# Sparse attention into a gated feed-forward on one core: batch 2's key transposes and value sums moved, two weight loads and two products halved

## The chip, the core and the metric

The kernel runs on one core of a Trainium2 chip. The core has TensorE (PE, with PEld for its weight loads), VectorE (DVE), ScalarE (ACT), GpSimd (POOL), SyncE (SP) and 16 DMA engines that all queues share. The metric is the time of one execution on the device in microseconds (us). A lower time is better.

## What is computed

Four batches, eight heads, 768 positions, head size 64. Each query attends to the positions nearer than 16 and to one summary per block of 32 positions: the key summary is the maximum over the block, the value summary the mean. The heads' outputs are put side by side into rows of 512 and go through a feed-forward with 2048 hidden units.

```python
k_sum = k.reshape(B, H, nb, block, D).max(axis=3)
v_sum = v.reshape(B, H, nb, block, D).mean(axis=3)
scores_l = np.where(np.abs(pos[:, None] - pos[None, :]) < 16, scale * q @ k.T, -1e9)
scores_s = scale * q @ k_sum.T + np.log(32)
a = softmax(concat([scores_l, scores_s]))
x = a @ concat([v, v_sum])
h = x @ w_in
out = (h * sigmoid(1.702 * h)) @ w_out
```

## The kernel before

The kernel is one long program in which each engine keeps the order in which its instructions are written; nothing reorders them. The order is written by hand, as lists of short step names.

**Stages of one batch.** A batch needs its keys, queries and values loaded, keys and queries turned (head size onto the partitions), the block maxima of the keys and the block sums of the values, then scores, exponential, mask, product with the values, normalization and a turn back. Then comes its feed-forward: the *hidden stage* (16 tiles of 128 hidden units, in two halves of 384 positions, each four matmuls and one gelu on ScalarE) and the *output stage* (21 products of 8 matmuls, three 128-row tiles t with seven products each, in the manner of Strassen, so that VectorE first makes sums of the gelu outputs (`gs`) and of the weights (`ws`)). `seq` orders those products; batch 0 has a shorter list `seq0`. The attention of batch b + 1 is laid beside the output stage of batch b: after each product the function `beside(b + 1, slot)` issues the steps that a table has for that slot, `plan1` for batch 1 and `plan` for the others.

**Names of the steps.** In `plan1` and `plan`: `s` scores of a pair of heads for one half, with the exponential; `m` mask; `v` values of two pairs; `x` turn back on TensorE, `d` by DMA; `t` query and `k` key transposes on TensorE; `j` block maxima and copies of keys (`rest_k`); `K`, `Q`, `V` loads of batch 2; `X` key transposes by DMA on SP's queue (`xk`); `R` the value sums (`value_rows`); `e` and `g` fetch ScalarE's table for the exponential or the gelu. In `XR`, the list for batch 0's second half: `m`, `l`, `o`, `r` hidden tiles; `y` the gelu of an `m` tile; `Pti` product i of tile t; `w`, `G`, `h` sums for the output stage.

**Value sums.** `value_rows(s)` issues on SP four copies of neighbouring rows within the value tile `vw[s]` (`vw<-vw`), 48 small matmuls on TensorE (`vsum`, tile ps_vs) that need all twelve value loads of the batch, five operations on VectorE (`block_sums`: vpart, vs), and on SP two copies of the sums into `vw[s]` (`vw<-vs`). The `v` steps read what these copies wrote. In batch 1's hidden stage it is issued for batch 2 at

```python
if n // 2 == (6 if b == 1 else 1):
    value_rows(s)
```

that is, behind 14 of 16 hidden tiles. For batch 3 it stands behind the first four tiles.

**Buffers.** Scores, transposes on TensorE, values and value sums share two PSUM buffers (`psb`); hidden tiles and products share three in batch 0 and four after it (`pmm`). Keys and queries are loaded into two buffers each (`kb`, `qb`).

**Queues.** POOL issues all loads from HBM, in order, and also makes the masks and some key copies. SP issues the stores of the output and all copies and transposes by DMA, in order. Weight loads: `w_in` in five parts, the last of them columns 1536 to 2048, and `w_out` in four quarters.

Of the kernel before, what the change touches and what calls it, by code (L numbers as in the profile page):

```python
# [35 lines left out]
def kernel(  # L36
# [10 lines left out]
    B, H, S, D = q.shape  # L47
# [196 lines left out]
        wi = moe_w_in.rearrange("(ko ki) n -> ki ko n", ki=128)  # L244
        pool.dma_start(out=w_in_sb[:, :, n0:n1], in_=wi[:, :, n0:n1])

    def load_w_out(rows, cols):
        n, m = NT // 2, d_model // 2
        wo = moe_w_out.rearrange("(nt ni) d -> ni nt d", ni=128)
        pool.dma_start(out=w_out_sb[:, rows * n:rows * n + n, cols * m:cols * m + m],  # L250
                       in_=wo[:, rows * n:rows * n + n, cols * m:cols * m + m])

    def copy(eng, out, in_):
        if eng is act:
# [502 lines left out]
        gelu("CBAE".index(bank) % 2, j + (NT // 2 if bank in "AE" else 0), ff_now[j, bank])  # L757


    def product(b, t, what):  # L760
        n = NT // 2
        l = slice(t * 128, t * 128 + 128)
        r = slice(HALF + t * 128, HALF + t * 128 + 128)
        lo, hi = slice(0, N1), slice(N1, d_model)
        raw_l, raw_r = gTb[:, :, l], gTb[:, :, r]
        w1, w2 = w_out_sb[:, 0:n], w_out_sb[:, n:]
        lhs, rhs, bank, opens = {
            1: (raw_l[:, 0:n], w1[:, :, lo], "A", True),
            2: (raw_l[:, n:], w2[:, :, lo], "C", True),
            6: (gs[:, 1, :, l], ws[:, 1], "A", False),  # L770
            5: (gs[:, 0, :, l], ws[:, 0], "B", True),
            7: (raw_r[:, 0:n], ws[:, 2], "A", False),
            3: (gs[:, 2, :, l], w2[:, :, hi], "B", False),
            4: (raw_r[:, n:], ws[:, 3], "A", False)}[what]
        if opens and b == 0 and bank == "A" and t == 0:
            now["left"] = pleft.tile([128, 512], F32, name="poA", tag="left")
        if opens:
            now[t, bank] = (last_bank("B" if bank == "A" and t == 2 else {"A": "A", "B": "E", "C": "C"}[bank],
                                      "po" + bank) if b + 1 == B
                            else now["left"] if b == 0 and bank == "A" and t < 2  # L780
                            else pmm.tile([128, 512], F32, name="po" + bank, tag="mm"))
        o = N1 if b == 0 and bank == "A" and t == 1 else 0
        po = now[t, bank][:, o:o + N1]
        for i in range(n):
            pe.matmul(out=po, lhsT=lhs[:, i], rhs=rhs[:, i], start=(opens and i == 0 and not o),
                      stop=(i == n - 1), skip_group_check=True)

        def keep_it(name):
            if b + 1 == B and name == "s1":
                t_ = now[t, name] = spare[:, 2 * HALF + t * N1:2 * HALF + (t + 1) * N1]  # L790
            else:
                t_ = now[t, name] = snap.tile([128, N1], F32, name=name, tag=name)
            copy(dve if t == 0 and 0 < b < B - 1 else act, t_, po)

        def give(o, cols, name):
            if (t, o) not in now:
                now[t, o] = outp.tile([128, d_model], F32, name="osb", tag="osb")
            if name:
                dve.tensor_tensor(out=now[t, o][:, cols], in0=po, in1=now[t, name], op=ALU.add)
            else:  # L800
                act.activation(out=now[t, o][:, cols], in_=po, func=ACT.Copy)

        def store(o, tok, cols=slice(0, d_model)):
            r0 = b * S + tok
            sp.dma_start(out=out[r0:r0 + 128, cols], in_=now[t, o][:, cols])
            if cols.start == 0:
                now.pop((t, o))

        last = b == B - 1 and t == JH - 1

        if what == 1 and (b or t == 2):
            keep_it("s1")
        elif what == 1:
            pass
        elif what == 2:
            give("o1", lo, "s1")
        elif what == 6:
            keep_it("s2")
        elif what == 5:
            keep_it("s5")  # L820
        elif what == 7:
            give("o2", hi, "s5")
            if last:
                store("o2", HALF + t * 128, hi)
        elif what == 3:
            give("o1", hi, "s2")
            store("o1", t * 128)
        else:
            give("o2", lo, None)
            store("o2", HALF + t * 128, lo if last else slice(0, d_model))  # L830
# [56 lines left out]
    w50 = vw[0].rearrange("p (j e) h c -> p j e h c", e=2)  # L887
    for a in range(NP):
        load_q1(a)
    load_w_in(1536, 2048)  # L890
    load_w_out(0, 0)
    load_w_out(1, 0)
    load_w_out(0, 1)
    finish_masks()
# [100 lines left out]
    for e in range(2):  # L995
# [4 lines left out]
    load_batch(1)  # L1000


    plan1 = {0: ['j0'], 1: ['j1'], 2: ['t1', 'e', 'K0'], 3: ['R', 'j2', 'K1'], 4: ['s00', 'Q0'], 5: ['s01', 's10', 'j3'], 6: ['m00', 'm01'], 7: ['t2', 's11', 'm10'], 8: ['t3', 'm11', 'Q1', 'V'], 9: ['s02', 's03'], 10: ['m02', 'm03'], 11: ['s12', 's13', 'X0'], 12: ['g', 'v00', 'v01'], 15: ['x00', 'm12'], 16: ['x01', 'm13', 'X1']}
    XE = {}

    plan = {-1: ["s00", "s01"], 2: ["m00", "m01"], 3: ["s02", "s03"], 5: ["m02", "m03", "s10", "s11"],
            7: ["m10", "m11", "s12", "s13"], 9: ["m12", "m13"], 10: ["v00", "v01"], 11: ["d00"],
            12: ["d01"], 13: ["v10", "v11"], 14: ["d10"], 15: ["d11"], 18: ["g"]}

    def beside(b, slot):  # L1010
        for what in (plan1 if b == 1 else plan).get(slot, ()):
            half, i = int(what[1:2] or 0), int(what[-1:] if len(what) > 1 else 0)
            if what[0] == "t":
                tq(i, 1, act)
            elif what[0] == "j":
                rest_k(i, 1, dve if i == 3 else pool)
            elif what[0] == "k":
                tk(i, 1, act)
            elif what[0] == "K":
                load_turned(k, 2, kb2, "kb", (i,))  # L1020
            elif what[0] == "Q":
                load_turned(q, 2, qb2, "qb", (i,))
            elif what[0] == "V":
                load_v(2)
            elif what[0] == "X":
                xk(i, 0)
            elif what[0] == "Y":
                xq(i, 0)
            elif what[0] == "m":
                mask(half, i)  # L1030
            elif what[0] == "g":
                gelu_soon()
            elif what[0] == "R":
                value_rows(1)
            elif what[0] == "e":
                exp_soon()
            elif what[0] == "s":
                scores(b, half, i)
            elif what[0] == "v":
                values(b, half, i)  # L1040
            elif what[0] == "d":
                dx(half, i)
            else:
                tx(half, i, XE.get((half, i), act))
# [11 lines left out]
    def run(steps):  # L1056

        for what in steps.split():
# [4 lines left out]
                scores(0, 1, i)  # L1063
                mask(1, i)
            elif what[0] == "P":
                product(0, i, int(what[2]))
            elif what[0] == "v":
                values(0, 1, i)
            elif what[0] == "x":
# [19 lines left out]
            elif what[0] == "N":  # L1089
                held[what[1:]] = pleft.tile([128, 512], F32, name="ph", tag="left")[:, 0:HALF]  # L1090
                ff_step(held[what[1:]], 0, int(what[1:]))
            elif what[0] == "y":
                gelu(0, int(what[1:]), held.pop(what[1:]))
            elif what[0] == "K":
                k_late(i, dve)
                key_halos(i, 0, dve, JH)
                key_rows(i, 0, ks0[:, i, 0:nb], dve, JH)
            elif what[0] == "C":
                dve.memset(vw[1][:, :, :, D:VC], 1.0)
                clear_values(dve, 1)  # L1100
            elif what[0] == "V":
                act.activation(out=gate3[:, 0:1], in_=gate[:, 0:1], func=ACT.Copy)
                vrows0()
            elif what[0] == "w":
                w_sum(i, int(what[2]))
            elif what[0] == "G":
                g_sums(i, dve, (0, 2, 1, 3), int(what[2]))
            elif what[0] == "h":
                g_sums(i, dve, (0, 1))
            elif what[0] == "k":  # L1110
                tk(i, 1, act)
            elif what[0] == "j":
                rest_k(i, 1, pool)
            elif what[0] == "t":
                tq(i, 1, act)
            else:
                value_rows(1)
# [4 lines left out]
    snap = ctx.enter_context(tc.tile_pool(name="snap", bufs=1, reuse_waits="tile"))  # L1122
    gs = snap.tile([128, 3, NT // 2, HALF], F16, name="gs")
    ws = keep.tile([128, 4, NT // 2, N1], F16, name="ws")
    XR = """m12 m13 m14 s2 s3 g P01 P11 y12 v0 y13 y14 v1 l15 S0 x0 P02 S1 x1 P12 o3 r9 w00 w01 r2 G02 w20 r10 w21 r3 r11 G22 r4 r12 k0 w10 w11 r5 r13 G42 k1 r6 r14 k2 t0 r7 r15 k3 G61 h7 w30 w31"""
    run(XR)
    def run1(steps):

# [14 lines left out]
    for b in range(0, B - 1):  # L1143
# [6 lines left out]
        if b:  # L1150
# [4 lines left out]
            for n in range(0, NT, 2):  # L1155
# [14 lines left out]
                if nxt:  # L1170
                    if n == 0 and b > 1:
                        pool.tensor_copy(out=gate2, in_=xTT[1][1][:, 1, 0:1])
                        load_turned(q, b + 1, qb2, "qb")
                    if n // 2 == (6 if b == 1 else 1):
                        value_rows(s)
                    if b == 1 and n // 2 in (0, 1):
                        xq(n // 2, s)
                    if b > 1 and n // 2 == 2 * b:
                        xq(0, s)
                        xq(1, s)  # L1180
# [108 lines left out]
```

## Time and profile before

| | us |
|---|---|
| three timed runs | 211.26, 211.11, 210.6 |
| median | 211.11 |
| the profiled execution, own time | 212.82 |
| its span, first to last instruction | 210.7 |
| TensorE busy in it | 199.3 |
| VectorE, ScalarE, POOL busy | 145.7, 130.9, 97.9 |
| mean granted clock of TensorE | 0.992 of full speed |

The profile is of one execution, and its times count from its first instruction. A row of a timeline reads: start, length, engine, line of the program, operation, out<-in, the shape and how many were merged; in brackets the idle time of that engine in front of it and what ended it. All recorded operations carry the helper's line L28, so tiles' names tell them apart. A row of the chain of waits has the start, the length and what the chain ran through. A row of the windows has the length, then the busy time and the instruction count of TensorE, its weight loads, VectorE, ScalarE and POOL, then the granted clock, the mean number of busy packets per DMA engine as a share, and GB/s. A row of DMA issues ends in KB each and the us from issue to landing. SP's rows are issues; a transfer lands later.

### The profile page before, as it was taken

To read this page: it belongs to the slowest core of one execution; us is meant where nothing else is said; L and a number is where in the kernel's file an instruction comes from. 1 tells how busy PE (TensorE), PEld (TensorE's weight loads), DVE (VectorE), ACT (ScalarE), POOL (GpSimd) and SP (SyncE) were. 2 spreads that over 40 slices of the span, in tenths; PEclk is the share of its full clock that TensorE was granted. 3 is DMA by queue.
4 is the path that set the end of the run, shared out by engine and by line. 5 is a ranking of instruction groups with operands and counts; after the bars stand their busy time and mean duration, and the time that the engine had idled before them with its cause. 6 is when DMAs were issued, how large, how long until landed. Compare 5 with 4: busy or idle time off the path is not lost.

```text
span 210.7 us, 6003 instructions
## 1 busy us (share of the span) xinstructions
PE 199.3 (95%) x2436; PEld 145.7 (69%) x2436; DVE 145.7 (69%) x369; ACT 130.9 (62%) x253; POOL 97.9 (46%) x157
## 2 busy tenths in 40 slices
PE   7899988999999999983999999999999999999993
PEld 7567646667778966551688885665888865568882
DVE  6877985779996832996576859898667554768221
ACT  2385879679778668760666156677781557985220
POOL 7975389556999212294696118000000008992000
PEclk9999999999999999998899999999999999999999
DMA  5999999999999999999899979999122950000222
GB/s 62 157 160 202 199 226 200 181 156 121 96 185 219 208 107 213 94 140 69 139 149 211 171 164 123 97 238 194 28 96 43 163 152 0 0 5 0 100 103 100
DMA packets 99179, 27.75 MB, mean 132 GB/s; under 512 B 86720, under 2 KB 96208, under 8 KB 99152
## 3 DMA queue, kind: packets, MB, share of 16 engines
q0 software_dynamic: 73520, 13.64, 84.8%
q1 hardware_dynamic: 25632, 13.74, 36.2%
q8 instruction: 19, 0.31, 0.7%
q14 instruction: 8, 0.07, 0.1%
HBM read 27.26 MB, written 6.29 MB: 159 GB/s over the span
## 4 chain that ended last, share of the span: by engine, by line
PE 55%; DMA 20%; POOL 9%; issue 7%; DVE 7%; ACT 0%; POOLq 0%; DVEq 0%
PE poA L28 16%; PE ph L28 16%; PE poB L28 8%; DMA w_out_sb<-in_moe_w_out_dram 7%; DMA kb<-in_k_dram 5%; PE poC L28 5%; DMA w_in_sb<-in_moe_w_in_dram 4%; DMA vw<-in_v_dram 4%; PE phA L28 4%; DVE gs L28 3%; POOL vw L28 2%; POOL kb L28 2%; POOL v0n L28 2%; PE ps_av L28 2%; PE ps_s L28 2%
## 5 line engine op out<-in xcount | busy, mean ns | idle before, releaser
L28 PE MATMUL ph<-xT,w_in_sb 128*128 128x384 f16 x416 | 72.2, 330 | 0.6 <-DMA w_in_sb<-in_moe_w_in_dram 0.5
L28 ACT ACTIVATE gT<-ph 128x384 f16<-128x384 f32 x104 | 49.5, 491 | 24.9 <-PE ph L28 24.5
L28 PEld LDWEIGHTS <-w_in_sb 128*128 128x128 f16 x452 | 43.8, 99 | 29.2 <-issue 1.9
L28 PEld LDWEIGHTS <-gT 128*128 128x128 f16 x384 | 36.2, 98 | 5.8 <-issue 0.8
L28 POOL DMA_DIRECT2D vw<-in_v_dram x36 | 24.6, 702 | 25.3 <-DMA qb<-in_q_dram 13.2
L28 PEld LDWEIGHTS <-gs 128*128 128x128 f16 x288 | 27.6, 98 | 3.6 <-DVE gs L28 0.2
L28 ACT ACTIVATE a_sb<-ps_s 128x768 bf16<-128x768 f32 (+1 forms) x32 | 24.9, 826 | 7.7 <-PE ps_s L28 7.7
L28 POOL TENSOR_TENSOR gs<-gT 128x384 f16<-128x384 f16 x7 | 6.4, 908 | 43.8 <-ACT gT L28 43.8
L28 PE MATMUL poA<-ws,gT 128*128 128x256 f16 x192 | 25.0, 273 | 0.1
L28 DVE TENSOR_TENSOR a_sb<-a_sb,mk 128x768 bf16<-128x768 bf16 x28 | 14.8, 553 | 4.7 <-ACT a_sb L28 4.1
L28 POOL DMA_DIRECT2D qb<-in_q_dram x18 | 16.6, 944 | 1.8 <-DMA v0n<-in_v_dram 1.5
L28 DVE TENSOR_TENSOR x<-ps_av,rc 128x768 f16<-128x768 f32 (+1 forms) x20 | 15.8, 796 | 0.6
L28 DVE TENSOR_TENSOR gs<-gT 128x384 f16<-128x384 f16 (+1 forms) x22 | 8.8, 401 | 10.0 <-ACT gT L28 9.8
L28 POOL DMA_DIRECT2D kb<-in_k_dram x16 | 15.3, 972 | 0.8 <-POOLq L1273 0.8
L28 ACT ACTIVATE osb<-poA 128x256 f32<-128x256 f32 x12 | 4.6, 384 | 16.1 <-PE poA L28 16.0
L28 ACT ACTIVATE s<-poA 128x256 f32<-128x256 f32 x17 | 6.6, 388 | 12.5 <-PE poA L28 11.9
L28 PEld LDWEIGHTS <-kx 64*128 64x128 bf16 (+1 forms) x372 | 9.3, 95 | 6.1 <-issue 3.5
L28 ACT ACT_TABLE_LOAD x10 | 12.8, 1283 | 1.0 <-PEq L1273 0.8
L28 PE MATMUL poA<-w_out_sb,gT 128*128 128x256 f16 x96 | 12.3, 273 | 0.6 <-DMA w_out_sb<-in_moe_w_out_dram 0.6
L28 PE MATMUL poB<-ws,gs 128*128 128x256 f16 x96 | 12.6, 273 | 0.0
L28 PE MATMUL poC<-w_out_sb,gT 128*128 128x256 f16 x96 | 12.5, 273 | 0.0
L28 PE MATMUL poA<-ws,gs 128*128 128x256 f16 x96 | 12.5, 273 | 0.0
(113 smaller groups left out, 300.9 us busy)
## 6 DMA issues: line engine op xcount, KB each, us to landing
out_dram<-osb SPq DMA_DIRECT2D x23, 256.0 KB, 2.6
kb<-in_k_dram POOLq DMA_DIRECT2D x16, 192.0 KB, 6.8
qb<-in_q_dram POOLq DMA_DIRECT2D x14, 192.0 KB, 11.2
vw<-in_v_dram POOLq DMA_DIRECT2D x36, 64.0 KB, 6.3
w_out_sb<-in_moe_w_out_dram POOLq DMA_DIRECT2D x4, 512.0 KB, 13.7
w_in_sb<-in_moe_w_in_dram POOLq DMA_DIRECT2D x3, 512.0 KB, 12.1
vw<-vs SPq DMA_DIRECT2D x6, 198.0 KB, 6.0
v0n<-in_v_dram POOLq DMA_DIRECT2D x4, 192.0 KB, 7.4
```

The lines of the kernel that those rows point to most:

```text
L28: r = f(*a, **kw)
```

## The change

Five edits, all in the order of work; no arithmetic is added or taken away.

1. The last part of `w_in` is loaded as two halves of 256 columns, the first quarter of `w_out` as two halves of four tiles.
2. Batch 0's first two products P01 and P11 are cut into halves of four matmuls. The first halves stand before the values v0, the second halves behind them; the gelus y12 to y14 are issued behind the second halves.
3. Batch 1's last key transpose (k3) moves from in front of the products to slot 2 of `plan1`; the query transpose t0 moves behind hidden tile r7. The sums of tiles 6 and 7 (G61, h7) are made in another order, those for the products 5 and 6 first.
4. The key loads K0 and K1 of batch 2 are issued one slot earlier and ahead of pair 2's copies. The key transposes X0 move from slot 11 to slot 16, beside X1, behind batch 0's last product. On SP they now stand behind two more stores of the output.
5. Batch 2's value sums move from batch 1's hidden stage to slot 1 of its output stage, by a new table `plan2` that otherwise equals `plan`.

```diff
-    def load_w_out(rows, cols):
+    def load_w_out(rows, cols, i0=0, i1=NT // 2):
         n, m = NT // 2, d_model // 2
         wo = moe_w_out.rearrange("(nt ni) d -> ni nt d", ni=128)
-        pool.dma_start(out=w_out_sb[:, rows * n:rows * n + n, cols * m:cols * m + m],
-                       in_=wo[:, rows * n:rows * n + n, cols * m:cols * m + m])
+        r, c = slice(rows * n + i0, rows * n + i1), slice(cols * m, cols * m + m)
+        pool.dma_start(out=w_out_sb[:, r, c], in_=wo[:, r, c])
...
-        for i in range(n):
+        for i in range(n) if part is None else range(part * n // 2, part * n // 2 + n // 2):
             pe.matmul(out=po, lhsT=lhs[:, i], rhs=rhs[:, i], start=(opens and i == 0 and not o),
...
-    load_w_in(1536, 2048)
-    load_w_out(0, 0)
+    load_w_in(1536, 1792)
+    load_w_in(1792, 2048)
+    load_w_out(0, 0, 0, 4)
+    load_w_out(0, 0, 4, 8)
...
-    plan1 = {0: ['j0'], 1: ['j1'], 2: ['t1', 'e', 'K0'], 3: ['R', 'j2', 'K1'], ..., 11: ['s12', 's13', 'X0'], ..., 16: ['x01', 'm13', 'X1']}
+    plan1 = {0: ['j0'], 1: ['j1', 'K0'], 2: ['t1', 'k3', 'e'], 3: ['R', 'K1', 'j2'], ..., 11: ['s12', 's13'], ..., 16: ['x01', 'm13', 'X0', 'X1']}
...
+    plan2 = {-1: ['s00', 's01'], 1: ['R'], 2: ['m00', 'm01'], ...}
...
             elif what[0] == "R":
-                value_rows(1)
+                value_rows(b % 2)
...
             elif what[0] == "h":
-                g_sums(i, dve, (0, 1))
+                for j, w in ((i - 1, 2), (i, 0), (i - 1, 1), (i, 1), (i - 1, 3)):
+                    g_sums(j, dve, (w,))
+            elif what[0] == "H":
+                g_sums(i, dve, (0,))
...
-    XR = """m12 m13 m14 s2 s3 g P01 P11 y12 v0 y13 y14 v1 l15 ... k2 t0 r7 r15 k3 G61 h7 w30 w31"""
+    XR = """m12 m13 m14 s2 s3 g P010 P110 v0 P011 P111 y12 y13 y14 v1 l15 ... k2 r7 t0 r15 H6 h7 w30 w31"""
...
-                    if n // 2 == (6 if b == 1 else 1):
+                    if b > 1 and n // 2 == 1:
                         value_rows(s)
```

More of the change, by code (lines that the diff above doesn't have):

```diff
@@ L757, in ff_gelu, with product @@
         gelu("CBAE".index(bank) % 2, j + (NT // 2 if bank in "AE" else 0), ff_now[j, bank])
-    def product(b, t, what):
+    def product(b, t, what, part=None):
         n = NT // 2
@@ L774, in product @@
             4: (raw_r[:, n:], ws[:, 3], "A", False)}[what]
+        opens = opens and part != 1
         if opens and b == 0 and bank == "A" and t == 0:
@@ L1000 @@
     load_batch(1)
-    plan1 = {0: ['j0'], 1: ['j1'], 2: ['t1', 'e', 'K0'], 3: ['R', 'j2', 'K1'], 4: ['s00', 'Q0'], 5: ['s01', 's10', 'j3'], 6: ['m00', 'm01'], 7: ['t2', 's11', 'm10'], 8: ['t3', 'm11', 'Q1', 'V'], 9: ['s02', 's03'], 10: ['m02', 'm03'], 11: ['s12', 's13', 'X0'], 12: ['g', 'v00', 'v01'], 15: ['x00', 'm12'], 16: ['x01', 'm13', 'X1']}
+    plan1 = {0: ['j0'], 1: ['j1', 'K0'], 2: ['t1', 'k3', 'e'], 3: ['R', 'K1', 'j2'], 4: ['s00', 'Q0'], 5: ['s01', 's10', 'j3'], 6: ['m00', 'm01'], 7: ['t2', 's11', 'm10'], 8: ['t3', 'm11', 'Q1', 'V'], 9: ['s02', 's03'], 10: ['m02', 'm03'], 11: ['s12', 's13'], 12: ['g', 'v00', 'v01'], 15: ['x00', 'm12'], 16: ['x01', 'm13', 'X0', 'X1']}
     XE = {}
@@ L1008 @@
             12: ["d01"], 13: ["v10", "v11"], 14: ["d10"], 15: ["d11"], 18: ["g"]}
+    plan2 = {-1: ['s00', 's01'], 1: ['R'], 2: ['m00', 'm01'], 3: ['s02', 's03'], 5: ['m02', 'm03', 's10', 's11'], 7: ['m10', 'm11', 's12', 's13'], 9: ['m12', 'm13'], 10: ['v00', 'v01'], 11: ['d00'], 12: ['d01'], 13: ['v10', 'v11'], 14: ['d10'], 15: ['d11'], 18: ['g']}
     def beside(b, slot):
-        for what in (plan1 if b == 1 else plan).get(slot, ()):
+        for what in (None, plan1, plan2, plan)[b].get(slot, ()):
             half, i = int(what[1:2] or 0), int(what[-1:] if len(what) > 1 else 0)
@@ L1065, in run @@
             elif what[0] == "P":
-                product(0, i, int(what[2]))
+                product(0, i, int(what[2]), int(what[3]) if what[3:] else None)
             elif what[0] == "v":
@@ L1124 @@
     ws = keep.tile([128, 4, NT // 2, N1], F16, name="ws")
-    XR = """m12 m13 m14 s2 s3 g P01 P11 y12 v0 y13 y14 v1 l15 S0 x0 P02 S1 x1 P12 o3 r9 w00 w01 r2 G02 w20 r10 w21 r3 r11 G22 r4 r12 k0 w10 w11 r5 r13 G42 k1 r6 r14 k2 t0 r7 r15 k3 G61 h7 w30 w31"""
+    XR = """m12 m13 m14 s2 s3 g P010 P110 v0 P011 P111 y12 y13 y14 v1 l15 S0 x0 P02 S1 x1 P12 o3 r9 w00 w01 r2 G02 w20 r10 w21 r3 r11 G22 r4 r12 k0 w10 w11 r5 r13 G42 k1 r6 r14 k2 r7 t0 r15 H6 h7 w30 w31"""
     run(XR)
@@ L1173 @@
                         load_turned(q, b + 1, qb2, "qb")
-                    if n // 2 == (6 if b == 1 else 1):
+                    if b > 1 and n // 2 == 1:
                         value_rows(s)
                     if b == 1 and n // 2 in (0, 1):
-                        xq(n // 2, s)
+                        xq(n // 2 - 0, s)
                     if b > 1 and n // 2 == 2 * b:
```

## The prediction

> **What bounds the kernel now.** I read the page's head first, then who TensorE waits for, then the chain of waits, then TensorE's own timeline with the granted clock where the chain leaves TensorE.
>
> ```profile
> span 210.7 us, 6003 instructions
> ...
> PE 199.3 (95%) x2436; PEld 145.7 (69%) x2436; DVE 145.7 (69%) x369; ACT 130.9 (62%) x253; POOL 97.9 (46%) x157
> ```
>
> TensorE is busy for 199.3 of 210.7 us, so a change that removes no matmul can only win what TensorE waits or runs slowly. The waits of TensorE alone (us in total, times, longest):
>
> ```profile
> PE ps_vs L28 <- DMA vw<-in_v_dram: 3.8, 5, 2.6
> ...
> PE poA L28 <- DMA w_out_sb<-in_moe_w_out_dram: 0.6, 1, 0.6
> PE ph L28 <- DMA w_in_sb<-in_moe_w_in_dram: 0.5, 1, 0.5
> ```
>
> The greatest is the value sums (tile ps_vs) on the load of the values. The next two are the two weight loads that the change halves. Which batch's sums it is, and what follows, stands in the chain (start, us, what) and, below it, in TensorE's timeline:
>
> ```profile
> 90.93 7.75 DMA vw<-in_v_dram
> ...
> 99.31 3.99 PE ph L28 x16
> 103.30 0.46 PE ps_s L28 x24
> 103.76 0.98 PE poA L28 x8
> 104.74 0.87 PE poB L28 x8
> ...
> 115.16 0.88 PE ps_av L28 x48
> ...
> 131.07 0.53 PE ps_vs L28 x48
> 131.60 15.72 PE ph L28 x96
> ```
>
> ```profile
> 93.68 0.36 PE L28 MATMUL ps_vs<-vw,E 64*32 64x128 bf16 x24
> ...
> 97.11 0.25 PE L28 MATMUL ps_vs<-vw,E 64*32 64x128 bf16 x7 [2.61 <-DMA vw<-in_v_dram]
> ```
>
> Batch 2's sums start at 93.68 in batch 1's hidden stage and crawl behind the landing values until about 99.3. The 16 hidden products after them then take 3.99 us, where 96 such take 15.72 (0.164 each, so 2.62 for 16). The windows say why (granted clock is the third number from the end):
>
> ```profile
> 98.00:100.00 2.00, 1.50 (x18) 0.75 (x18) 0.58 (x3) 0.00 (x0) 0.00 (x0) 0.62 0.00 0
> 100.00:102.00 2.00, 2.00 (x8) 0.92 (x7) 1.80 (x4) 0.49 (x1) 0.08 (x1) 0.53 0.75 122
> ```
>
> The clock lost 0.38 of 2 us and 0.47 of 2 us, as at half rate for 3.4 us, directly after the starved stretch. [...]
>
> **The change part by part**, against the profiled execution's 212.82 us (span 210.7, 2.1 around it); the timed runs' median, 211.11, is 1.7 lower.
>
> *A. The sums leave the hidden stage.* From 93.68 to 103.30 are 9.62 us; what stays there is 16 products, 2.62. Saved: **7.0**, of which 3.99 - 2.62 = 1.4 is clock. I cannot tell from one trace whether the 1.7 us faster timed runs pay that 1.4; I count half, so **6.3**, with 5.6 and 7.0 as ends.
>
> *B. The sums enter batch 1's output stage* behind its second product: 48 matmuls, 0.53 (the row at 131.07). They need one of two score buffers (psb), both just taken by the scores in front. ScalarE's timeline shows when the first comes free:
>
> ```profile
> 105.25 1.49 ACT L28 ACTIVATE a_sb<-ps_s 128x768 bf16<-128x768 f32 x2
> ```
>
> The first of two exponentials ends near 106.0, 2.7 after the stage's start at 103.30; TensorE is there after 0.46 + 0.98 + 0.87 = 2.3. So a wait of 0.4, and B costs **0.9**. VectorE's part (evacuation and block sums, about 1.5 by the row below) also moves here. VectorE reaches the stage late by about as much as that 0.4, so I add nothing:
>
> ```profile
> 97.16 0.40 DVE L28 TENSOR_TENSOR gs<-gT,gs 128x384 f16<-128x384 f16 x1
> ...
> 99.69 1.18 DVE L28 TENSOR_TENSOR vs<-ps_vs,vpart 32x128 bf16<-32x128 f32 x4
> ```
>
> ```profile
> L28 DVE TENSOR_REDUCE ks<-kx 128x24 bf16<-128x768 bf16 x12 | 11.3, 946 | 0.1
> ```
>
> Its work ends at 97.56 before; with the sums gone it goes on at once with a maximum (0.95) and the first of the last sums (0.40), to 98.4 with part C's shift of 0.5. Product 5 needs that for its last matmul, near 95.8 + 2.3 = 98.1.
>
> *C. Halved weight loads and products.* At most three waits go, 0.6 and 0.5 of the list and 0.2 below: 1.3. But what is late next is ScalarE:
>
> ```profile
> 33.05 1.51 ACT L28 ACTIVATE a_sb<-ps_s 128x768 bf16<-128x768 f32 x2 [0.29 <-PE ps_s L28]
> 34.58 1.28 ACT L28 ACT_TABLE_LOAD   x1
> ```
>
> ```profile
> 36.51 0.81 PE L28 MATMUL ph<-xT,w_in_sb 128*128 128x384 f16 x4
> 37.55 0.51 PE L28 MATMUL ps_x<-ident,x 128*128 128x128 f16 x6 [0.23 <-DVE x L28]
> ```
>
> The hidden tile 15 at 36.51 needs the buffer that the first gelu behind this table load frees, and exponentials and table load can come only 0.29 earlier, the idle time in front of them. With the 0.23 on VectorE, which the earlier values remove, C gains **0.5** (ends 0 and 1.3). The price is on POOL's queue:
>
> ```profile
> 25.37 0.87 POOL L28 DMA_DIRECT2D w_out_sb<-in_moe_w_out_dram  x1 [1.67 <-DMA w_in_sb<-in_moe_w_in_dram]
> ...
> 31.40 0.23 POOL L28 TENSOR_SCALAR_AFFINE_SELECT mk<-mk 32x64 bf16<-32x64 bf16 x1
> ```
>
> ```profile
> 32.16 1.19 DVE L28 TENSOR_TENSOR a_sb<-a_sb,mk 128x768 bf16<-128x768 bf16 x2 [0.72 <-ACT a_sb L28]
> ```
>
> POOL waited here for an older load's landing before it issued the next; two more issues, 0.87 each at most, put the mask building, done at 31.63, some 1.1 later, as the waits shrink by part of it. The multiplications by the masks began at 32.16 and are then done at 32.7 + 1.2 = 33.9; the values v0 come behind two half products (0.9 together, as half of two products of 0.87) and want them at about that time. Behind POOL's masks the batch 1 loads also stand; the DMA queue is deep there, so I cost them at nothing, 0.5 if not. [...] The 256 KB loads of this trace were issued 0.75 us apart and landed 8.2 us (median) after issue, so they overlap; the sum goes by that:
>
> ```profile
> w_in_sb<-in_moe_w_in_dram POOLq DMA_DIRECT2D x2, 256.0 KB, 8.2
> ```
>
> *D. Key pair 3 of batch 1 and the regrouped sums:* six transposes and one ScalarE copy move behind two products, still ahead of their use; batch 2's key loads are issued ahead of pair 2's POOL copies, which the scores six products further on need. Zero; a wait there, or one that goes, is bounded by the 0.23 above, so 0.3 either way.
>
> *E. Batch 2's key transposes* move past two output stores on SP:
>
> ```profile
> 67.57 3.64 SPq L28 DMA_TRANSPOSE kx<-kb  x2
> ...
> 74.51 4.80 SPq L28 DMA_TRANSPOSE kx<-kb  x2
> 83.28 8.82 SPq L28 DMA_TRANSPOSE qT<-qb  x2
> 98.87 2.69 SPq L28 DMA_DIRECT2D vw<-vw  x4
> 101.65 1.51 SPq L28 DMA_DIRECT2D vw<-vs  x2
> ```
>
> All four then stand together from about 74.0 to 82.4 (3.64 + 4.80 behind 74.51 less part C), still ahead of the query transposes, which waited for their loads until 83.28. The first landed 10.8 after issue, at 94.1:
>
> ```profile
> qT<-qb SPq DMA_TRANSPOSE x1, 10.8
> ```
>
> The scores after the change want it at 103.30 - 7.0 - 0.5 = 95.8. Zero, with 1.7 us to spare.
>
> *F. The sums' way back.* The two copies vw<-vs, issued at 101.65 to 103.16 before the stage began, now come inside it, beside batch 3's key loads; beside batch 2's, one took 7.1:
>
> ```profile
> vw<-vs SPq DMA_DIRECT2D x1, 198.0 KB, 7.1
> ```
>
> Sums end about 3.3 into the stage, VectorE 4.8, second copy issued 5.7, landed 12.8. Values v00 ran 115.16 - 103.30 = 11.9 into the stage, now 0.9 later, 12.8. No slack; I charge **0.4** (ends 0 and 2).
>
> *G. Batch 3.* Its query transposes are just in time:
>
> ```profile
> 140.82 5.94 SPq L28 DMA_TRANSPOSE qT<-qb  x2
> ```
>
> ```profile
> qT<-qb SPq DMA_TRANSPOSE x1, 6.4
> ```
>
> 140.82 + 6.4 = 147.2 against TensorE at 131.60 + 15.72 = 147.3. Their chain hangs on batch 2's output transposes, hence on TensorE, so it shifts along; batch 3's loads hang on batch 2's query transposes too and may shift by less. Zero (end +1.5, a quarter of the shift).
>
> Sum: -6.3 + 0.9 - 0.5 + 0.4 = **-5.5**. Against 212.82 that is 207.3; against the median, **205.6**.
>
> **The rivals.**
>
> *R1, the query transposes become the bound.* They queue behind four key transposes in one block instead of two and two. If each holds SP as long as the slowest, 3.4 (below), 13.6 us from 74.0 put the query transposes at 87.6 instead of 83.28; the first lands at 98.4 and the scores wait 2.6: 208.2. For it: a query transpose took 10.8 to land here and 6.4 in batch 3, so transfers already crowd each other; against it: the query loads go ahead of the moved transposes and should land earlier.
>
> ```profile
> L28 SPq DMA_TRANSPOSE kx<-kb x4: 1305/1769/3401, 67.6 to 75.9; - x4
> ```
>
> *R2, slower: VectorE sits behind a late key transpose.* The maxima of pairs 2 and 3 stand on VectorE's ordered queue in front of the last sums that product 5 needs. They have until about 95 (97.56 less a maximum and four sums). If the second pair of transposes, issued last and beside all value loads, lands at 101, over twice the 10.8 above after its issue near 78, VectorE is 6 late, TensorE idles 6 and pays the half clock again (1.4): 205.6 + 7.4 = 213.0. It decides from a landing near 99. For it: VectorE's order is fixed and it ended the stage late already; against it: it takes a landing that no row shows.
>
> *R3, the values bound the stage.* If the loads still land at 98.7 (90.93 + 7.75), the halo copies hold SP until 101.6 as before, the second sum copy follows at 102.5 and lands at 109.6; v00 wants it at 95.8 + 12.8 = 108.6. That is 1.0 late, or 4.7 if it takes the 10.8 of the transposes on the same queue; in the middle, for 0.4 charged already: 205.6 - 0.4 + 2.8 = 208.0.
>
> *R4, it doesn't do what it says:* the values land only after 101, TensorE waits as before but in the output stage: 211.
>
> **How the numbers follow.** The forecast, 205.6, has 0.58; R1 0.12, R3 0.12, R4 0.04, R2 0.14. The forecast's own range is 204.0 (A full and C at 0.9) to 207.3 (A at 5.6, F and G half-way to their ends). The range 203.8 to 209.8 takes in R1 and R3 with 1.6 us of doubt and leaves out R2, R4. Faster by over 0.3% (0.6 us, about what a measurement of this kernel can tell): 0.82; the same: 0.04; slower: 0.14.
>
> **What would show it.** Right: no ps_vs wait near 95, granted clock 1.00 through that stage, the scores of batch 2 at about 96, a wait of about 0.4 before ps_vs on ScalarE, batch 3's first scores near 141 to 142, front gain at the ps_x of 37.55 about 0.5. Wrong: TensorE idle over 1 us before the scores (R1), before product 5 on VectorE's gs (R2), before ps_av (R3), or before ps_vs on the value load again (R4).

## The result and the profile after

The changed kernel takes **208.00 us** (median of six runs, 207.63 to 208.59). Six runs of the kernel before on the same chip have a median of 210.86 us (209.54 to 212.46). The ratio is **0.9868, 95% interval 0.9823 to 0.9913**: faster by 2.9 us. The forecast was 205.6, with a range of 203.8 to 209.8: the direction was right, the gain was about half of what the sum gave. The profiled execution took 207.85 us, that of the kernel before 212.82. Medians below are over all runs, while ratios and their intervals leave out a kernel's runs more than 1.5% above its fastest (19 of 57 of the kernel before, 6 of 12 of the front alone), so that a median and a ratio can point apart where the time varies.

The head of the page of the changed kernel, and the waits of TensorE (us in total, times, longest):

```profile
span 205.8 us, 6003 instructions
...
PE 196.5 (95%) x2436; PEld 144.6 (70%) x2436; DVE 143.2 (70%) x369; ACT 131.0 (64%) x253; POOL 101.2 (49%) x159
```

```profile
PE ps_t L28 <- DMA qb<-in_q_dram: 1.6, 1, 1.6
...
PE ps_vs L28 <- ACT a_sb L28: 0.5, 1, 0.5
...
PE ps_s L28 <- DMA qT<-qb: 0.2, 1, 0.2
```

The value sums (ps_vs) wait for the value loads no more, and the two weight loads of the front are gone from the list too. A new wait stands at its top: the query transposes (ps_t) of batch 1 on the last load of their queries. TensorE is busy for 2.8 us less with the same 2436 instructions; the half clock that is gone is part of that. TensorE's timeline shows each step in its place:

```profile
36.79 0.50 PE L28 MATMUL ps_x<-ident,x 128*128 128x128 f16 x6
...
62.67 0.49 PE L28 MATMUL ps_t<-wide,qb 128*128 128x128 bf16 x6 [1.61 <-DMA qb<-in_q_dram]
...
74.50 1.79 PE L28 MATMUL ph<-xT,w_in_sb 128*128 128x384 f16 x10
...
97.06 0.52 PE L28 MATMUL ps_s<-qT,kx 64*128 64x64 bf16 x24
99.92 0.60 PE L28 MATMUL ps_vs<-vw,E 64*32 64x128 bf16 x48 [0.48 <-ACT a_sb L28]
...
110.10 0.95 PE L28 MATMUL ps_av<-vw,a_sb 128*64 128x65 bf16 x48
...
120.71 1.46 PE L28 MATMUL ph<-xT,w_in_sb 128*128 128x384 f16 x8
...
142.53 0.53 PE L28 MATMUL ps_s<-qT,kx 64*128 64x64 bf16 x24 [0.21 <-DMA qT<-qb]
```

And of the kernel before, the starts of the same two hidden stages:

```profile
73.73 2.44 PE L28 MATMUL ph<-xT,w_in_sb 128*128 128x384 f16 x14
...
125.70 1.46 PE L28 MATMUL ph<-xT,w_in_sb 128*128 128x384 f16 x8
```

The stretch from batch 1's hidden stage to batch 2's hidden stage took 125.70 - 73.73 = 52.0 us before and 120.71 - 74.50 = 46.2 us after. All of the gain lies in this stretch, 5.8 us, and 0.8 were lost ahead of it (74.50 against 73.73). Its granted clock (third number from the end) is full where it was 0.62 and 0.53 before:

```profile
98.00:100.00 2.00, 1.52 (x28) 1.21 (x32) 1.35 (x4) 1.99 (x4) 2.00 (x4) 1.00 0.04 8
100.00:102.00 2.00, 2.00 (x63) 1.77 (x63) 1.36 (x5) 0.57 (x1) 2.00 (x3) 1.00 1.55 99
```

What I had not looked for stands on the queues. SP's rows after the change, and POOL's rows for the last value loads of batch 2, first before, then after:

```profile
75.28 8.66 SPq L28 DMA_TRANSPOSE kx<-kb  x4
84.05 7.86 SPq L28 DMA_TRANSPOSE qT<-qb  x2
92.12 2.69 SPq L28 DMA_DIRECT2D vw<-vw  x4
102.10 1.25 SPq L28 DMA_DIRECT2D vw<-vs  x2
```

```profile
79.44 0.68 POOL L28 DMA_DIRECT2D vw<-in_v_dram  x1 [4.57 <-DMA qb<-in_q_dram]
83.56 0.68 POOL L28 DMA_DIRECT2D vw<-in_v_dram  x1 [3.45 <-DMA qb<-in_q_dram]
88.03 0.68 POOL L28 DMA_DIRECT2D vw<-in_v_dram  x1 [3.79 <-DMA qb<-in_q_dram]
88.93 3.39 POOL L28 DMA_DIRECT2D vw<-in_v_dram  x5 [0.22 <-issue]
```

```profile
79.50 1.36 POOL L28 DMA_DIRECT2D vw<-in_v_dram  x2
81.48 0.68 POOL L28 DMA_DIRECT2D vw<-in_v_dram  x1 [0.62 <-DMA vw<-in_v_dram]
82.81 0.68 POOL L28 DMA_DIRECT2D vw<-in_v_dram  x1 [0.66 <-DMA vw<-in_v_dram]
```

Before, POOL could not issue the value loads: it waited three times for about 4 us for *query* loads to land. These waits are the program's own: in the trace POOL's loads use eight semaphores in turn to tell that they have landed, and a value load waits until the load eight before it, the last to use its semaphore, has landed. The query loads issued from 63.46 on landed at 78.91, 83.27 and 87.75, and the value loads above followed at 79.44, 83.56 and 88.03. After, the last value load goes out at 82.81 instead of about 91.6, and it lands at 91.2 instead of 99.0, by the trace's DMA issues (its row after the change, the last number in us from issue to landing):

```profile
vw<-in_v_dram POOLq DMA_DIRECT2D x1, 64.0 KB, 8.4
```

So the values were there about 3 us before the sums' *old* place, which would lie near 94.5 in this execution. Moving the sums may not have been needed at all. The query loads show the same, in the DMA issues from 63 to 75.2 us (x, KB each, median us from issue to landing), with the packets of POOL's queue (q0: packets, MB, share); before, then after:

```profile
q0 software_dynamic: 7884, 1.00, 129.7%
...
qb<-in_q_dram POOLq DMA_DIRECT2D x4, 192.0 KB, 20.5
```

```profile
q0 software_dynamic: 9578, 1.21, 169.1%
...
qb<-in_q_dram POOLq DMA_DIRECT2D x4, 192.0 KB, 11.1
```

### The profile page after: what moved, and what is told of

It is laid out like the page before. It is cut to its first block, busy times and chain, and to the rows that moved or that the text cites. A ratio compares the mean times of both kernels' runs of the same rounds, so it can differ in the third digit from the quotient of the medians.

```text
span 205.8 us, 6003 instructions
## 1 busy us (share of the span) xinstructions
PE 196.5 (95%) x2436; PEld 144.6 (70%) x2436; DVE 143.2 (70%) x369; ACT 131.0 (64%) x253; POOL 101.2 (49%) x159
## 4 chain that ended last, share of the span: by engine, by line
PE 54%; DMA 23%; POOL 13%; SPq 3%; issue 2%; DVE 2%; ACT 1%; POOLq 0%; DVEq 0%
PE poA L28 17%; PE ph L28 11%; DMA qb<-in_q_dram 9%; PE poB L28 8%; DMA w_in_sb<-in_moe_w_in_dram 6%; DMA kx<-kb 4%; PE poC L28 4%; PE phA L28 4%; DMA qT<-qb 4%; POOL kb L28 3%; SPq L28 3%; PE ps_av L28 3%; PE ps_s L28 2%; POOL mk L28 2%; POOL v0n L28 2%
## 5 line engine op out<-in xcount | busy, mean ns | idle before, releaser
L28 PE MATMUL ph<-xT,w_in_sb 128*128 128x384 f16 x416 | 70.9, 326 | 0.1
L28 ACT ACT_TABLE_LOAD x10 | 12.8, 1283 | 1.0 <-PEq L1281 0.8
```

Source lines behind the costliest of these rows:

```text
L28: r = f(*a, **kw)
```

## The experiments

**Theory S**, the one of the prediction: the gain comes from the sums' new place. **Theory T**, the rival: two key transposes on SP's queue beside the loads hold the loads up; moved away, they let the values land in time, and the sums' place does not matter. **Theory L**: the earlier front is given back through the late query load. In the table, "stretch" is the time from batch 1's to batch 2's hidden stage in the one profiled execution, as worked out above, and the ratio is that to the kernel before on the same chip.

| kernel | keys moved | sums moved | front | median us | ratio, 95% interval | stretch us |
|---|---|---|---|---|---|---|
| before, the two profiles | no | no | no | 211.4 (57 runs) | 1 | 52.0, 50.8 |
| front alone | no | no | yes | 212.01 | 0.9968, 0.9915 to 1.0021 | 49.5 |
| sums alone | no | yes | no | 210.26 | 0.9912, 0.9860 to 0.9963 | 47.8 |
| keys alone | yes | no | no | 207.45 | 0.9822, 0.9773 to 0.9872 | 46.2 |
| keys alone, again | yes | no | no | 207.68 | 0.9858, 0.9807 to 0.9910 | 46.0 |
| all but the keys | no | yes | yes | 209.60 | 0.9938, 0.9891 to 0.9985 | 46.2 |
| all but the sums | yes | no | yes | 207.36 | 0.9849, 0.9798 to 0.9901 | 46.2 |
| all but the front | yes | yes | no | 207.40 | 0.9831, 0.9788 to 0.9873 | 46.7 |
| neither sums nor front | yes | no | no | 207.83 | 0.9868, 0.9820 to 0.9917 | 46.2 |
| all (the changed kernel), again | yes | yes | yes | 208.14 | 0.9873, 0.9812 to 0.9935 | 46.2 |
| one of the two keys moved | half | no | no | 212.35 | 1.0066, 1.0022 to 1.0110 | 49.4 |

"All but" and "neither" rows keep the reordered key steps and sums of the change's third and fourth edit; "alone" rows have none of them.

**Sums alone.** The kernel before with

```diff
+    plan2 = {-1: ['s00', 's01'], 1: ['R'], 2: ['m00', 'm01'], ...}
-        for what in (plan1 if b == 1 else plan).get(slot, ()):
+        for what in (None, plan1, plan2, plan)[b].get(slot, ()):
-                    if n // 2 == (6 if b == 1 else 1):
+                    if b > 1 and n // 2 == 1:
```

> The kernel before with the value sums of batch 2 moved to the output stage of batch 1 and nothing else changed. Theory S (moving the sums out of the hidden stage is what removes the stall): the values still land near 98.7 us, the hidden stage ends near 97, the sums come about 2.3 us behind it and wait at most 0.5 us for the values; hidden stage some 22.6 us instead of 29.5, output stage 23.5 to 24 instead of 22.5; time 206 to 207.5. Rival T (moving the key transposes is what removes it, because the loads then land some 7 us earlier; the sums' new place is not needed): the sums in the output stage wait for the values again, over 1 us on tile ps_vs, and the values v00 wait for the copies of the sums; time 208.5 to 211.

Its SP row for the copies within the value tile, which need all value loads, and TensorE's waits behind it:

```profile
98.00 3.46 SPq L28 DMA_DIRECT2D vw<-vw  x4
```

```profile
97.17 0.35 PE L28 MATMUL ps_s<-qT,kx 64*128 64x64 bf16 x12 [0.70 <-POOL kx L28]
...
110.78 0.92 PE L28 MATMUL ps_av<-vw,a_sb 128*64 128x65 bf16 x47 [1.07 <-DMA vw<-vs]
```

210.26, ratio 0.9912. The values still land near 98, the sums do not wait for them (99.30 in the timeline), and the hidden stage is as short as theory S has it, 22.55 us (73.56 to 96.11). But other things come late: the copies of the sums (1.07 us at ps_av), and in front a POOL copy of the keys (0.70), so that the output stage takes 25.25 us where S had 23.5 to 24. Between the theories, with the time in T's range: half a gain, and the profiled execution (209.14) was one of the quick ones.

**Keys alone.**

```diff
-    11: ['s12', 's13', 'X0'], ... 16: ['x01', 'm13', 'X1']
+    11: ['s12', 's13'],       ... 16: ['x01', 'm13', 'X0', 'X1']
```

> The kernel before with the first two key transposes of batch 2 moved from slot 11 to slot 16 and nothing else changed; the sums stay in the hidden stage. Theory T (the transposes on SP's queue hold up the loads; out of the way, the values land near 91 as in the changed kernel, before the sums' old place near 94): no wait of ps_vs for the values, hidden stage 23 us, output stage as before (22.5), time 205.5 to 207. Theory S (the sums' place decides): the values land later than 94 and the sums wait 1 us or more; time 209 to 211.

SP's rows, the sums in TensorE's timeline, and the query loads in the same window as above:

```profile
75.38 8.49 SPq L28 DMA_TRANSPOSE kx<-kb  x4
...
92.80 2.69 SPq L28 DMA_DIRECT2D vw<-vw  x4
```

```profile
94.56 0.60 PE L28 MATMUL ps_vs<-vw,E 64*32 64x128 bf16 x48
```

```profile
q0 software_dynamic: 9118, 1.16, 151.8%
...
qb<-in_q_dram POOLq DMA_DIRECT2D x4, 192.0 KB, 11.2
```

207.45, ratio 0.9822: **as large a gain as that of the whole change, from one step name moved by five slots.** The query loads land after 11.2 us instead of 20.5, the values at 92.2 instead of 99.0, and the sums in their old place wait for nothing. Theory T's account holds, with a time about 0.5 us above its range; S falls, for the sums need not move once the transposes have.

**All but the front.** `load_w_in(1536, 2048)`, `load_w_out(0, 0)` and `P01 P11 y12 v0` put back.

> The changed kernel without its front: last part of w_in and first quarter of w_out loaded whole again, products P01 and P11 whole and in the old order before v0. Theory L (the earlier front pulls the copies of the sums onto the DMA engines ahead of batch 1's last query load, which makes the query transposes t2 wait 1.6 us, so the front loses 0.8 by the start of the next hidden stage): the wait of ps_t for qb near 62 goes, the hidden stage of batch 1 starts near 73.8 instead of 74.5, time 0.5 to 1 lower than the changed kernel's 208.0, so 207 to 207.5. Rival (the front's 0.76 us is kept, the late query load has another cause, such as batch 1's order of key loads): time 208 to 208.8 and the wait of 1.6 stays.

207.40; no wait of ps_t for the query load. As theory L says, but the hidden stage began at 74.28 where L had 73.8, and the difference to the changed kernel is within the intervals.

**Front alone.** The kernel before with those halves only.

> The kernel before with the halved weight loads and the halved products alone. Theory L: the first values and the turn back come about 0.7 us earlier (ps_x of batch 0 near 36.8 instead of 37.55), then the query transposes t2 of batch 1 wait about 1.6 us for their load; start of batch 1's hidden stage 0.3 to 0.8 later than 73.73; time 210.9 to 211.7 where the kernel before has 210.9. Rival: the 0.76 us is kept to the end: 210.1 to 210.4.

212.01, ratio 0.9968, interval across 1. The turn back came early here too, but batch 1's hidden stage began at 73.38 and the 1.61 us were not there. Of the five profiles with the front one has that wait, and another 0.3 us of it; in none of the eight without does t2 wait for its load by 0.2 us or more. So the front alone does not bring it. Theory L is not borne out, its rival neither: the front's worth can't be told from nothing.

**The kernel before, profiled once more.**

> The kernel before, unchanged, profiled once more: does what TensorE loses in front of batch 2's value sums stay the same from run to run? Theory V (it varies, and with it the granted clock): the values land at another time than 98.96 us, the wait of ps_vs for them is not 3.8 us, and the time goes with it, 209.5 with a clock of 1.00 to 214 with 0.984. Rival: the same wait of 3.8 within 0.3 us, 211 to 213, clock 0.992.

```profile
96.34 0.25 PE L28 MATMUL ps_vs<-vw,E 64*32 64x128 bf16 x7 [2.07 <-DMA vw<-in_v_dram]
...
97.41 0.96 PE L28 MATMUL ps_vs<-vw,E 64*32 64x128 bf16 x15 [0.15 <-DMA vw<-in_v_dram]
```

211.67 us; 2.7 us of waits where the first profile had 3.8, and a stretch of 50.8 instead of 52.0. As theory V has it, the stall is not of a fixed size; the granted clock was 0.992 again, though, and the time lies where the rival had it too. The front-alone kernel, whose stall is the same piece of program, had 2.7 us of it too but no half clock, and a stretch of 49.5.

**All but the sums**, then **all but the keys**, then **neither sums nor front** (the edits above, undone in the changed kernel).

> The changed kernel with the value sums of batch 2 put back into batch 1's hidden stage; key transposes moved, front kept. Theory T (the moved transposes alone removed the stall, the sums' new place only costs): no wait of ps_vs for the values, no wait of 0.48 us on ScalarE, hidden stage 23.2 us, output stage 22.5; 0.5 to 1.0 less than the changed kernel, 207.0 to 207.6. Theory S (the sums had to go too): the sums wait for the values by 1 us or more; 209 or more.

> The changed kernel with the first two key transposes of batch 2 put back at slot 11; front and moved sums kept. Theory T: the values land after 97 us again, the output stage waits on tile ps_vs, on kx or on the sums' copies (ps_av) for 1 to 2 us together, and the time varies as with the sums alone: 209.5 to 211. Theory S: as the changed kernel, 207.6 to 208.5.

> The changed kernel with the sums back in the hidden stage and without the halved loads and products: what is left is the moved key transposes and the reordered key steps. Theory T with L (the transposes give all of the gain, the front and the sums' new place each cost 0.5 to 0.8): 206.3 to 207.0, the fastest of all. Rival (the front and the sums cost nothing by themselves; each of the two lower times before it was chance): 207.4 to 208.0.

All but the sums, 207.36: the sums in their old place cost nothing, so T again. All but the keys, 209.60, with single runs from 207.42 to 213.32: with the keys in the old place the time is worse and scattered, as T says. Its profiled execution, one of the quickest (207.81, last value at 96.6), has the same stretch of 46.2 and in it only the changed kernel's wait of 0.48 us, not the 1 to 2 us that T named, so no trace shows where its longer runs lose their time. Neither sums nor front, 207.83: my expectation of 206.3 to 207.0 was a miss, and with it the idea that front and sums each cost 0.5 to 0.8.

**One of the two transposes moved.**

```diff
-    def xk(g, s):
+    def xk(g, s, es=(0, 1)):
...
-        for e in range(2):
+        for e in es:
...
-    11: ['s12', 's13', 'X0'], ... 16: ['x01', 'm13', 'X1']
+    11: ['s12', 's13', 'X0'], ... 16: ['x01', 'm13', 'Z0', 'X1']
...
-                xk(i, 0)
+                xk(i, 0, (0,) if i == 0 else (0, 1))
+            elif what[0] == "Z":
+                xk(i, 0, (1,))
```

> The kernel before with only the second of the two early key transposes moved to slot 16; the first stays at slot 11. Theory T, transposes beside the loads hold them up in proportion: the last value load lands between the 98.0 to 99.0 us of two early transposes and the 91 to 92 us of none, 94 to 96, so that the sums near 94 wait for it by less than 1.5 us; time 208 to 210. Rival, any transpose early does it (the loads are held up once, not in proportion): last landing 97 or later, wait over 1.5 us, time 210 to 212.

```profile
96.92 0.30 PE L28 MATMUL ps_vs<-vw,E 64*32 64x128 bf16 x7 [1.93 <-DMA vw<-in_v_dram]
```

```profile
q0 software_dynamic: 7959, 1.01, 133.0%
...
qb<-in_q_dram POOLq DMA_DIRECT2D x4, 192.0 KB, 12.9
```

The loads gain in part (queries after 12.9 us, last value at 96.9, between 92 and 99), the time gains nothing: 212.35, ratio 1.0066. The sums stand at 94.4 and want all values then; a landing at 96.9 is still a stall, and the mean granted clock was 0.981 to 0.992 in 11 of 12 runs. Theory T's numbers missed in all three (landing, wait, time); the rival had the wait and came within 0.4 of the rest, but the query loads did gain with each transpose moved, as T has it. Why this kernel is somewhat slower than the kernel before stays open.

**The changed kernel and the keys alone, once more, on one chip.**

> The changed kernel once more, on the same chip as the next. Theory N (once the key transposes are moved, the front and the sums' place change nothing that can be told): within 0.5 us of the kernel with the key transposes alone, so 207.3 to 208.2, and the wait of 1.61 us for the query load in front of t2 is not there each time. Rival C (they cost 0.5 to 1.0): above it by that, and the 1.6 us are there again.

> The kernel before with the first two key transposes at slot 16 and nothing else, once more, on the same chip as the changed kernel. Theory N: 207.2 to 208.0, the same as the changed kernel within 0.5. Rival C: 206.8 to 207.3, below the changed kernel by 0.5 to 1.0.

```profile
61.75 0.49 PE L28 MATMUL ps_t<-wide,qb 128*128 128x128 bf16 x6 [0.46 <-ACT s L28]
...
142.83 0.53 PE L28 MATMUL ps_s<-qT,kx 64*128 64x64 bf16 x24 [0.88 <-DMA qT<-qb]
```

208.14 and 207.68; the rows are of the changed kernel, and its query load was in time here. Theory N holds: no version with the moved keys beats the others by more than can be told. The best medians, 207.4 to 207.7, are those of kernels simpler than the changed one.

## Why the prediction was right and wrong

**The bound** was read rightly: TensorE's starved value sums and the half clock behind them. All of the gain lies there.

**A, the sums leave the hidden stage**: 7.0 in the trace was forecast, and the hidden stage went from 29.5 us (73.73 to 103.23) to 22.6 (74.50 to 97.06): 6.9. The size was right, and the move alone does it: sums alone, with the values still late, has a hidden stage of 22.55. What A left out is that the wait would have gone without it. In keys alone the sums stay, and the stage is 23.19 us, longer only by about the sums' own work; with the keys moved the stretch is 46.2 us with the sums in either place.

**B, the sums in the output stage**: 0.9 forecast, with a wait of 0.4 behind ScalarE; the wait is 0.48 and the stage 1.2 longer (22.47, then 23.65). Right in kind, 0.3 too small. It is also why the sums' move is worth nothing once the keys are moved: the hidden and the output stage take 23.19 and 22.99 us in keys alone, 22.6 and 23.65 in the changed kernel, 46.2 together both times.

**C, the front**: 0.5 forecast, 0.76 seen at ps_x (37.55, then 36.79), and then lost. Over all profiles ps_x comes at 36.8 to 37.4 us with the halves (five, median 37.1) and at 37.3 to 38.3 without them (eight, median 37.6), so the 0.5 was there; but batch 1's hidden stage began at 73.4 to 74.8, with the halves or without them. I had priced the loads behind POOL's longer list at "nothing, 0.5 if not"; the chip shows a load that is late by 1.6 us in one execution and not in the next. The masks came later than the sum had them, too, though this cost nothing:

```profile
33.23 1.97 DVE L28 TENSOR_TENSOR a_sb<-a_sb,mk 128x768 bf16<-128x768 bf16 x4 [1.75 <-POOL mk L28]
```

**D** cannot be told from zero in the medians, as forecast. (Of the two key loads in this part only K0 comes a slot earlier; K1 stays in slot 3 and moves ahead of pair 2's copies.) One thing was overlooked: in five of the six profiles of kernels with these reordered steps TensorE stands idle for 0.2 to 1.4 us in front of a product between 70.8 and 71.8 us, with no wait recorded, and in none of the seven without them. What it waits for there is open.

**E, the key transposes, zero** is the step whose *working* failed. I asked only whether they would land in time for the scores. I did not ask what they had been doing to the loads that run beside them, although R1 noted that the query loads "should land earlier". Two rows show one such stretch, the DMA engines from 76.8 to 78.1 us, before and after (the last two numbers: mean busy packets per engine, GB/s):

```profile
76.80:78.10 1.30, 1.30 (x43) 0.97 (x36) 1.03 (x2) 0.40 (x2) 0.00 (x0) 1.00 0.25 8
```

```profile
76.80:78.10 1.30, 1.30 (x52) 0.94 (x51) 0.26 (x2) 1.17 (x4) 0.43 (x1) 1.00 2.09 225
```

Before, with query and value loads and four key transposes issued and not landed, the engines moved 8 GB/s. A stretch of 1.3 us with 8 to 13 GB/s between 66 and 82 us is in three of the five profiles with both transposes early. In all but the keys the lowest has 141, and the query loads still landed after 16.0 us, so such a stretch is not the whole of the delay. POOL's rows then show the chain: query loads late, so POOL's next value loads issued late, so values late. The packets point the same way: from 63 to 75.2 us POOL's queue moved 7038 to 8059 packets in the six profiles with a transpose early, 8718 to 9945 in the seven with none. The count does not set the landing, though: one of two had 7959 packets and query loads after 12.9 us, the kernel before 7884 and 20.5. Nor does it account for the 1.3 us at 8 GB/s. What held loads and transposes up is open.

**F, the sums' way back**: the forecast was a second copy landing 12.8 us into the stage, when v00 wants it. It landed at 109.81, 12.75 into it, and v00 at 110.10 did not wait. The 0.4 charged was too much here; all but the front waited 0.34 for it and sums alone 1.07. Without slack, as said.

**G, batch 3**: zero forecast with an end of 1.5; 0.21 in the changed kernel, 0.88 in its second profile.

**The step that made 205.6 too low** is the last one, "against the median, 205.6". Against its own execution the sum was good: 212.82 - 5.5 = 207.3, measured 207.85, 5.0 less. Part of that is luck, for misses cancelled: A gave 0.6 more than the sum had and F cost 0.4 less, B cost 0.3 more, and ahead of batch 1's hidden stage 0.8 was lost where C had 0.5 won. I then took the same 5.5 from a median 1.7 lower, as if all runs paid the stall of that execution, save half of the half clock. They don't. The mean granted clock of the 57 runs of the kernel before that shared chips with the experiments lies in groups: 16 runs at full clock (0.999 or more) with a median of 209.7 us, 26 near 0.992 with 211.5, 15 at 0.984 and below with 213.3. No profile was taken of an execution of the first group or the last. A step of 0.008 of 210 us is 1.7 us, what 3.4 us at half rate cost in the rows from 98 to 102 us. The changed kernel ran at 0.998 or more in 11 of 12 runs, median 208.1. So an execution of the kernel before at full clock is 1.6 us longer (209.7 to 208.1), which I put down to the rest of the stall less the 1.2 of B, and one near 0.992 is 1.8 longer still (211.5). What the change removes is the part that varies (57 runs of the kernel before take 208.87 to 215.29 us, 12 of the changed kernel 206.99 to 208.59); the sum's end, 207.3, was the better forecast of the median than the sum's difference.

**The range** holds 208.0 by luck: it reaches that far for R1 and R3, and neither came. The forecast's own range was also added up wrongly. By the ends that it names, A full and C at 0.9 give 204.5, not 204.0, and A at 5.6 with F and G half-way to their ends gives 207.9, not 207.3.

**The rivals.** R1 and R2 did not come: the scores at 97.06 wait for nothing, nor does product 5. R4 did not either. R3 came true where its condition held: in sums alone the values landed near 98, and ps_av waited 1.07 for the copy, where R3 had 1.0 to 4.7; the median there, 210.26, is above R3's 208.0.

## What to carry to other kernels

Before a step that waits for a load is moved, ask why the load is late: follow its issue (what POOL waited for) and then what shares the DMA engines with it. One issue moved off a crowded stretch did here what five edits did. Where a profile shows a stall, take the sum from that execution's own time and read its end, not its difference, against a median: a stall that varies from run to run is only partly in the median. And a transfer must make its date: here half-way earlier was worth nothing.

## What I had not expected of the hardware

**Loads landed 5 to 10 us later beside early transposes by DMA.** With both issued early, beside the query loads, these landed after 16.0 to 20.5 us at the median (five profiles), with one after 12.9, with none after 10.5 to 11.4 (seven profiles). It is not a rule for every load: in the changed kernel four key transposes stand beside the value loads, and these landed after 8.7 us at the median, where they took 9.1 before.

**TensorE's clock fell behind a gap of 1.93 us in one profile, and not behind one of 2.04 us in another.** In the kernel with one transpose moved, the longest gap was 1.93 us, and half rate followed (busy time of TensorE is the second number, the clock the third from the end):

```profile
94.00:95.00 1.00, 0.98 (x45) 0.51 (x43) 0.95 (x2) 0.84 (x2) 0.29 (x1) 1.00 1.53 168
95.00:96.00 1.00, 0.00 (x0) 0.00 (x0) 0.90 (x3) 0.04 (x1) 0.99 (x3) 1.00 1.62 128
96.00:97.00 1.00, 0.09 (x7) 0.08 (x6) 0.77 (x3) 0.00 (x0) 0.57 (x2) 0.95 0.74 87
97.00:98.00 1.00, 1.00 (x10) 0.47 (x10) 0.67 (x3) 0.00 (x0) 0.00 (x0) 0.50 0.79 153
...
100.00:101.00 1.00, 1.00 (x7) 0.57 (x6) 0.00 (x0) 0.57 (x2) 1.00 (x3) 0.84 0.87 182
```

The clock is at half rate for 0.1 + 3.0 + 0.32 = 3.4 us, 96.9 to 100.3; in the 3.4 us before, TensorE was busy for about 1.5. The two profiles of the kernel before, with longest gaps of 2.61 and 2.07 us, lose as much: 1.7 us of clock each, as at half rate for 3.4 us, the second of them from 97.5 to 100.9. The front-alone kernel had a gap of 2.04, and its granted clock was 1.00 in every microsecond from 93 to 103. So the length of the longest gap did not decide it here. The same program differs from run to run, too: the kernel before has a mean clock of 0.999 or more in 16 of its 57 runs, near 0.992 in 26, 0.984 and below in 15. What decides it is open.
